# A bank per feature tile for the small products, their sums formed in attention, and the ends of both layers woven

## The chip, the cores and the metric

One core of a Trainium2 chip runs the whole kernel. The metric is the device time of one execution in microseconds, the median of the runs shown. Names of engines are those of the profile: PE is TensorE's matmul, PEld its weight load, DVE VectorE, ACT ScalarE, POOL GpSimd, SP the engine that issues the DMAs.

## The reference, cut to what matters

Two batches of 768 tokens with 8 heads of 64 go through retention (a linear attention with a decaying state), then through two feed-forward layers without residuals:

```python
state = gamma * state + einsum('bhd,bhe->bhde', k[:, :, t], v[:, :, t])
y[:, :, t] = scale * einsum('bhd,bhde->bhe', q[:, :, t], state)
# x = y as 1536 tokens x 512 features
h = x @ w_in                          # 512 x 2048
x = (h * tanh(softplus(h))) @ w_out   # 2048 x 512
gate = 1 / (1 + exp(-(x @ w_gate)))   # 512 x 1536
out = (gate * (x @ w_val)) @ w_out2   # 1536 x 512
```

Everything is float32.

## The kernel before, in words

**Precision.** A float32 operand is split into two parts of PE's reduced type, a high copy (ACT, line 93) and the low rest (a subtraction on POOL or DVE, line 94; lines 195 and 196 for weights). A product of two operands is three matmuls (`mm3`: high x high, high x low, low x high). So a product over 256 input features is six matmuls of 128x128 weights.

**Tiling.** The 1536 tokens are three chunks of N = 512. The 16 blocks of 128 features of layer 1 and the 12 of layer 2 (gate and value) are taken in pairs of output rows. Chunks 1 and 2 are taken together with a seven-product scheme in place of eight (`pair_steps`): steps p1 to p7, each six matmuls, on sums of the inputs (tiles T1, T2, T3, T4 and the plain blocks B11, B21, B22) and sums of the weights (keys "s", made on POOL by lines 205 to 208). DVE forms the results from the products (lines 340, 345, 356, 365, 370). This is the "main" part; its matmuls are 128x512 and its results lie in four PSUM banks named "h". Chunk 0 is treated alike within itself: its two halves of H = 256 tokens form the pair. This is the "side" part; the profile names its products "hx", its matmuls are 128x256, its input sums are the tiles Y, and the profile prints YT for them. The inputs B11, B21, T4 and B22 of the side part are regions of the tile xc. In the old kernel all four side results lie in one PSUM tile "x" of two banks (line 388): bank 0 holds b1 and bA, bank 1 holds bB and b2, and a finished feature is read across both.

**After a product.** In layer 1, ACT applies Mish (line 429); in layer 2, ACT takes the gate's sigmoid (line 434) and DVE multiplies (line 438). The result is split into high and low (tile g). The output sums ("o", `o1` in layer 1, `o2` in layer 2) are six matmuls each over a pair of features in one of two PSUM banks, added to the accumulator of the chunk by DVE (lines 453 and 467), the first of a layer copied by ACT (lines 451 and 465).

**Order.** PE's order is the program's. Until attention's last block, all engines keep the program's order (`InOrder`); behind it the scheduler orders ACT, DVE and POOL from a simulation when it builds the program, and each engine then works through its own list in order. Attention runs in twelve blocks (`blocks`, lines 622 to 639): in block j come the scores of j+1, a decode step of the weights (`pump`), the state and output of j, POOL's preparation of j+2 (vp, og), the loads, and from block 4 on one plain product of layer 1's first four features ("dense"). Behind attention come output sums of chunk 0, plain products of chunk 2, output sums of chunk 1, and then the rounds: `three` issues main step k, side step k-1 and a share of the output sums of the round before (line 524). At k = 6 the last two side steps, p4 and p3, stand right behind each other. `weave` (line 515) spreads a list over another.

**Weights** come as packed words by SP's DMAs (two staging buffers), are decoded by ACT and DVE (lines 104 to 107), and are put into the rings "w" (7 buffers), "o" (4) and "q" (2) as they come free.

**Lines that the steps touch.** Side input sums of layer 1: line 670, once attention's buffers have gone. End of layer 1: lines 685 to 691, round 7's side part alone with four output sums, then its main part with eight, four of which (`out1(L1 - 1, 0, 4)`) join two pairs of features in one group of 12 matmuls; then `put_plain` (splits of chunk 0 for layer 2). Layer 2: lines 692 to 713, with rounds 2 to 10 in `three` and round 11's side and main parts one behind the other.

Of the kernel before, what the change touches and what calls it, by code (L numbers as in the profile page):

```python
# [23 lines left out]
def kernel(ctx, tc, qk, nv, w1i, w1o, w2g, w2v, w2o, ma_in, og_in, sg_in, ck_in, out):  # L24
# [52 lines left out]
    rings = {r: ctx.enter_context(tc.tile_pool(name="ring_" + r, bufs=n)) for r, n in RINGS.items()}  # L77
# [12 lines left out]
    y_t = {"B11": xc_t[:, :2, :, :H], "B21": xc_t[:, 2:, :, :H], "T4": xc_t[:, :2, :, H:], "B22": xc_t[:, 2:, :, H:]}  # L90
# [86 lines left out]
    def room(ring):  # L177
        own = owner[ring]
        n = len(own)
        return n < RINGS[ring] or left[own[n - RINGS[ring]]] == 0  # L180
# [94 lines left out]
    def put_sums(x0, x1, bt, cols, eng):  # L275

        def new(n):
            return up.tile([P, cols], F32, tag="u" if cols == N else "v", name=n)
# [22 lines left out]
    def side_sums():  # L301
        return put_sums(acc_t[0][:, :, :H], acc_t[0][:, :, H:], y_t, H, pool)
# [8 lines left out]
    def pair_steps(key, cols, bt, bank, done, late=False):  # L311
# [16 lines left out]
        def u(n):  # L328
            r[n] = up.tile([P, cols], F32, tag="u" if cols == N else "v", name=n)
            return r[n]  # L330
# [44 lines left out]
    PLACE = {(0, 0): "b1", (0, 1): "bB", (1, 0): "bA", (1, 1): "b2"}  # L375
# [5 lines left out]
    def side_steps(key, done):  # L381

        x = []
# [14 lines left out]
    def plain_steps(key, done, halves=None, own=False):  # L398

        x = []  # L400

        def one(i):
            if not own:
                o = hbank()
            elif "wide" not in hx:
                o = hbank() if i else hx["pool"].tile([P, N], F32, tag="x", name="hx")
            else:
                if not x:
                    x.append(hx["pool"].tile([P, 2, N], F32, tag="x", name="hx"))
                o = x[0][:, i]  # L410
# [113 lines left out]
    def three(main, side, outs, n=7):  # L524

        q = len(outs)
        for k in range(7):
# [5 lines left out]
            run(outs[(q * k + n - 1) // n:(q * k + q + n - 1) // n])  # L533


    with ExitStack() as actx:
# [4 lines left out]
        hx["pool"] = actx.enter_context(tc.tile_pool(name="ps_e", bufs=1, space=PSUM))  # L541
# [79 lines left out]

        def blocks(j0, dense, made):

            for j in range(j0, j0 + SPC):
# [12 lines left out]
                if dense:  # L637
                    dense.pop(0)()
            run(dense)
# [21 lines left out]
    dcs = ctx.enter_context(tc.tile_pool(name="dcs", bufs=1))  # L661
    ps_x = ctx.enter_context(tc.tile_pool(name="ps_x", bufs=1, space=PSUM))
    hx["pool"] = hx["wide"] = ps_x
# [3 lines left out]
    for n in ("T1", "T2", "T3"):  # L667
        y_t[n] = big2.tile([P, 2, 2, H], F32R, tag="y" + n, name="Y" + n)

    put_t4(side_sums(), y_t, pool)  # L670
# [24 lines left out]
    ts = side_sums()  # L695
    run(plain2(1))
    put_t4(ts, y_t, pool)
# [3 lines left out]
    for f in range(2, FF2):  # L701
# [4 lines left out]
        if f < FF2 - 1:  # L706
            three(seq(main_steps((2, f), done)), seq(side_steps((2, f), done)), rest[:n])
        else:
# [60 lines left out]
```

## Time and profile before

| | |
|---|---|
| median of 3 runs | 659.43 us (657.8 to 659.87) |
| profiled execution | 659.44 us, span 657.4 us |
| PE busy | 596.8 us (91%) |
| PEld busy | 495.1 us (75%) |
| DVE busy | 413.0 us (63%) |
| ACT busy | 295.0 us (45%) |
| POOL busy | 350.7 us (53%) |
| mean granted clock of TensorE | 0.966 |

Times of the trace are microseconds from the span's start. A row of the timeline gives start, duration, engine, line, operation, what it writes and reads, the shapes, the count, and in brackets the idle time of the engine just before it with what ended it. Matmuls are pipelined and their ends are modelled, so the spacing of starts is the better measure of a matmul's cost. The granted clock is 1.0 for 2.4 GHz and 0.5 for 1.2 GHz.

### The profile page before, as it was taken

To read this page: it belongs to the slowest core of one execution; us is meant where nothing else is said; L and a number is where in the kernel's file an instruction comes from. 1 tells how busy PE (TensorE), PEld (TensorE's weight loads), DVE (VectorE), ACT (ScalarE), POOL (GpSimd) and SP (SyncE) were. 2 spreads that over 40 slices of the span, in tenths; PEclk is the share of its full clock that TensorE was granted. 3 is DMA by queue.
4 is the path that set the end of the run, shared out by engine and by line. 5 is a ranking of instruction groups with operands and counts; after the bars stand their busy time and mean duration, and the time that the engine had idled before them with its cause. 6 is when DMAs were issued, how large, how long until landed. Compare 5 with 4: busy or idle time off the path is not lost.

```text
span 657.4 us, 8752 instructions
## 1 busy us (share of the span) xinstructions
PE 596.8 (91%) x3342; PEld 495.1 (75%) x3342; DVE 413.0 (63%) x581; ACT 295.0 (45%) x533; POOL 350.7 (53%) x299
## 2 busy tenths in 40 slices
PE   8999676797999999988978988999999999998897
PEld 7888565586878787877856766888888888887786
DVE  4899797127647474647578584457667666555255
ACT  1465736338353535345455473653453353331110
POOL 4375684229474747246793695745665575451000
PEclk9999989797999999999998996999999999999799
DMA  9982212004212020104130041013102221000004
GB/s 351 370 294 71 92 65 90 7 8 150 69 33 97 32 97 32 65 0 129 33 95 1 17 141 68 33 57 103 64 33 97 64 66 65 0 1 1 0 33 160
DMA packets 15593, 52.30 MB, mean 80 GB/s; under 512 B 1984, under 2 KB 2112, under 8 KB 15552
## 3 DMA queue, kind: packets, MB, share of 16 engines
q1 hardware_dynamic: 14976, 51.39, 22.6%
q8 instruction: 26, 0.43, 0.3%
q10 hardware_dynamic: 576, 0.36, 0.2%
q14 instruction: 15, 0.12, 0.1%
HBM read 48.60 MB, written 3.15 MB: 79 GB/s over the span
## 4 chain that ended last, share of the span: by engine, by line
PE 61%; DVE 14%; POOL 11%; DMA 5%; ACT 4%; issue 4%; SPq 0%; DVEq 0%; ACTq 0%; POOLq 0%
PE o L68 27%; PE h L68 22%; PE hx L68 11%; POOL g L94 3%; DMA raw<-w1i 3%; POOL ww L196 2%; POOL wo L196 2%; DVE T L94 1%; DVE a L68 1%; DVE v L68 1%; DVE raw L68 1%; DMA raw<-w2o 1%; DVE h L370 1%; DVE v L107 1%; DMA qk_t<-qk 1%
## 5 line engine op out<-in xcount | busy, mean ns | idle before, releaser
L68 PE MATMUL o<-g,wo 128*128 128x512 f32 x576 | 146.1, 403 | 25.6 <-ACT acc L451 19.2
L94 POOL TENSOR_TENSOR g<-e,g 128x512 fp32r<-128x512 f32 x74 | 104.3, 1414 | 86.9 <-ACT g L93 82.5
L68 PEld LDWEIGHTS o<-g,wo 128*128 128x128 f32 x576 | 109.4, 195 | 50.7 <-ACT acc L451 20.4
L68 PE MATMUL o<-wo,g 128*128 128x512 f32 x432 | 113.1, 399 | 6.0 <-POOL g L94 3.4
L68 PEld LDWEIGHTS o<-wo,g 128*128 128x128 f32 x432 | 79.9, 193 | 22.2 <-POOL g L94 4.6
L68 PE MATMUL h<-B,ww 128*128 128x512 f32 x372 | 95.9, 395 | 0.0
L196 POOL TENSOR_TENSOR ww<-s,ww 128x512 fp32r<-128x512 f32 x32 | 43.2, 1350 | 97.5 <-ACT ww L195 97.5
L68 PE MATMUL h<-T,ww 128*128 128x512 f32 x360 | 92.6, 394 | 0.8 <-DVE u L345 0.8
L68 PEld LDWEIGHTS h<-B,ww 128*128 128x128 f32 x372 | 69.6, 190 | 14.9 <-DVE h L356 0.4
L68 PEld LDWEIGHTS h<-T,ww 128*128 128x128 f32 x360 | 68.2, 190 | 15.6 <-DVE u L345 1.4
L68 PE MATMUL hx<-xc,ww 128*128 128x256 f32 (+1 forms) x336 | 58.4, 313 | 19.3 <-ACT e L429 11.3
L106 DVE SCALAR_TENSOR_TENSOR raw<-raw 128x512 int32<-128x512 int32 x59 | 54.4, 922 | 32.8 <-ACT raw L104 32.7
L107 DVE SCALAR_TENSOR_TENSOR v<-v,raw 128x512 int32<-128x512 int32 x59 | 59.4, 1007 | 23.5 <-ACT v L105 23.1
L68 PEld LDWEIGHTS hx<-xc,ww 128*128 128x128 f32 x336 | 50.4, 197 | 28.8 <-ACT e L429 13.1
L104 ACT ACTIVATE raw<-raw 128x512 int32<-128x512 uint8 x59 | 39.5, 670 | 70.0 <-DMA raw<-w1i 18.9
L453 DVE TENSOR_TENSOR acc<-o,acc 128x512 f32<-128x512 f32 x68 | 46.1, 684 | 28.5 <-PE o L68 28.4
L467 DVE TENSOR_TENSOR acc<-o,acc 128x512 f32<-128x512 f32 x60 | 41.2, 686 | 31.6 <-PE o L68 31.5
L93 ACT ACTIVATE g<-e 128x512 fp32r<-128x512 f32 x77 | 47.9, 625 | 17.3 <-DVE e L438 16.8
L105 ACT ACTIVATE v<-raw 128x512 f32<-128x512 f32 x59 | 39.3, 666 | 34.1 <-POOL s L208 17.7
L68 PEld LDWEIGHTS hx<-YT,ww 128*128 128x128 f32 x288 | 41.5, 196 | 7.7 <-ACT s L335 1.8
L196 POOL TENSOR_TENSOR wo<-v,wo 128x512 fp32r<-128x512 f32 x24 | 35.6, 1486 | 21.7 <-ACT wo L195 21.7
L68 PE MATMUL hx<-YT,ww 128*128 128x256 f32 x288 | 44.0, 290 | 2.6 <-ACT s L335 1.4
(102 smaller groups left out, 790.4 us busy)
## 6 DMA issues: line engine op xcount, KB each, us to landing
raw<-w1i SPq DMA_DIRECT2D x16, 512.0 KB, 3.4
raw<-w1o SPq DMA_DIRECT2D x16, 512.0 KB, 3.3
qk_t<-qk SPq DMA_DIRECT2D x12, 512.0 KB, 5.9
nv_t<-nv SPq DMA_DIRECT2D x12, 512.0 KB, 6.8
raw<-w2g SPq DMA_DIRECT2D x12, 512.0 KB, 3.3
raw<-w2v SPq DMA_DIRECT2D x12, 512.0 KB, 3.3
raw<-w2o SPq DMA_DIRECT2D x12, 512.0 KB, 3.3
out<-acc SPq DMA_DIRECT2D x12, 256.0 KB, 2.0
```

The source lines that it names most:

```text
L68: i = call(**kw)
L93: act.activation(out=hi, in_=raw, func=AF.Copy)
L94: eng.tensor_tensor(out=lo, in0=raw, in1=hi.bitcast(F32), op=ALU.subtract)
L104: act.activation(out=low, in_=rest, func=AF.Copy, scale=1.0 / 32, bias=-15.5 / 32)
L105: act.activation(out=v, in_=high.bitcast(F32), func=AF.Copy, scale=2.0 ** -112)
L106: dve.scalar_tensor_tensor(out=low, in0=high, scalar=SIGN, in1=low, op0=ALU.bitwise_and, op1=ALU.bitwise_or)
L107: dve.scalar_tensor_tensor(out=b, in0=b, scalar=3, in1=low, op0=ALU.logical_shift_left, op1=ALU.bitwise_or)
L196: late_lo.append(lambda: lo_eng["w"].tensor_tensor(out=lo, in0=v, in1=hi.bitcast(F32), op=ALU.subtract))
L370: dve.tensor_tensor(out=r["bB"], in0=r["bB"], in1=r["u2"], op=ALU.add)
L453: dve.tensor_tensor(out=acc, in0=o, in1=acc, op=ALU.add)
L467: dve.tensor_tensor(out=acc, in0=o, in1=acc, op=ALU.add)
```

## The change

There are five edits.

1. The side part's four results get a tile and a bank for each feature of the pair: x0 holds b1 and bB, x1 holds bA and b2. A finished feature is one whole bank. The plain products use the same two tiles.
2. The side input sums of layer 1 are formed in attention. `side_sums` now returns steps that run on POOL (with high copies on ACT); two steps follow each of blocks 5 to 9. Their tiles Y lie in memory that exists from the start, with scratch of their own (`upv`), and the ring "q" is made only after attention.
3. Layer 1's last round runs in `three` with the eight output sums of chunks 1 and 2, followed by `out1(L1 - 1, 0)` and `out1(L1, 0)` as groups of six matmuls.
4. In layer 2's round 2 the four output sums start at step 3.
5. Layer 2's last round runs in `three` with three output sums; what is left follows, then chunks 1, 0 and 2.

```diff
-    y_t = {"B11": xc_t[:, :2, :, :H], ...}
+    y_t = {n: big.tile([P, 2, 2, H], F32R, name="Y" + n) for n in ("T1", "T2", "T3")}
+    y_t |= {"B11": xc_t[:, :2, :, :H], ...}
...
     def side_sums():
-        return put_sums(acc_t[0][:, :, :H], acc_t[0][:, :, H:], y_t, H, pool)
+        x0, x1 = acc_t[0][:, :, :H], acc_t[0][:, :, H:]
+        t = {}
+        def form(n, k, in0, in1, to=None):
+            if to is None:
+                to = upv.tile([P, H], F32, tag="u", name="ty")
+            pool.tensor_tensor(out=to, in0=in0, in1=in1, op=ALU.subtract)
+            t[n, k] = to
+            if n != "T4":
+                low(n, k)
+        def low(n, k):
+            split(t[n, k], y_t[n][:, k, 0], y_t[n][:, k, 1], pool)
+        steps = []
+        for k in range(2):
+            steps += [lambda k=k: form("T1", k, x1[:, k], x0[:, k]),
+                      lambda k=k: form("T2", k, x1[:, 2 + k], t["T1", k]),
+                      lambda k=k: form("T4", k, x0[:, 2 + k], t["T2", k], t["T2", k]),
+                      lambda k=k: form("T3", k, x1[:, 2 + k], x1[:, k], t["T1", k])]
+        return steps + [lambda k=k: low("T4", k) for k in range(2)]
...
         def bank(n):
-            if not x:
-                x.append(hx["pool"].tile([P, 2, 2, H], F32, tag="x", name="hx"))
-            return x[0][:, int(n[1] in "B2"), int(n[1] in "A2")]
+            m, c = SPOT[n]
+            if m not in x:
+                x[m] = hx["pool"].tile([P, N], F32, tag=f"x{m}", name="hx")
+            return x[m][:, c * H:c * H + H]
...
-                done(m, 0, lambda m: x[0][:, :, m])
+                done(m, 0, lambda m: x[m])
...
-    def three(main, side, outs, n=7):
+    def three(main, side, outs, n=7, after=0):
...
-            run(outs[(q * k + n - 1) // n:(q * k + q + n - 1) // n])
+            run(outs[max(q * (k - after) + n - 1, 0) // n:max(q * (k - after + 1) + n - 1, 0) // n])
...
+        ys = side_sums()
...
+                if j >= SPC + 1:
+                    run(ys[:2])
+                    del ys[:2]
...
-    put_t4(side_sums(), y_t, pool)
...
-    for i in range(I0, L1):
-        three(seq(main_steps((1, i), mish_of(i))), seq(side_steps((1, i), mish_of(i))), rest, 3 if i == I0 else 7)
+    for i in range(I0, L1 + 1):
+        n = len(rest) if i < L1 else 8
+        three(seq(main_steps((1, i), mish_of(i))), seq(side_steps((1, i), mish_of(i))), rest[:n], 3 if i == I0 else 7)
+        run(rest[n:])
         rest = out1(i, 1) + out1(i, 2) + out1(i, 0)
-    weave(seq(side_steps((1, L1), mish_of(L1))), rest[:4])
-    weave(seq(main_steps((1, L1), mish_of(L1))), rest[4:8] + out1(L1 - 1, 0, 4))
+    run(out1(L1, 0))
...
-        if f < FF2 - 1:
-            three(seq(main_steps((2, f), done)), seq(side_steps((2, f), done)), rest[:n])
-        else:
+        if f == FF2 - 1:
             lo_eng["g"] = dve
-            weave(seq(side_steps((2, f), done)), rest[:3])
-            weave(seq(main_steps((2, f), done)), rest[3:6] + out2(f // 2, 0))
+            n = 3
+        three(seq(main_steps((2, f), done)), seq(side_steps((2, f), done)), rest[:n], 4 if f == 2 else 7, 3 if f == 2 else 0)
         rest = rest[n:]
-    run(out2(FF2 // 2 - 1, 1), out2(FF2 // 2 - 1, 2))
+    run(rest, out2(FF2 // 2 - 1, 1), out2(FF2 // 2 - 1, 0), out2(FF2 // 2 - 1, 2))
```

## Rows read from the trace of the kernel before

**Rows 1.** Windows: stretch, its length, busy us per engine (instructions), PEclk, DMA share, GB/s.
```profile
28.50:71.00 42.50, 42.50 (x469) 34.44 (x469) 37.39 (x47) 24.68 (x46) 22.78 (x17) 1.00 0.51 179
71.00:127.70 56.70, 37.52 (x146) 29.78 (x145) 40.96 (x44) 30.14 (x59) 34.89 (x31) 0.85 0.20 65
...
288.80:306.00 17.20, 13.73 (x79) 11.44 (x80) 10.45 (x16) 10.45 (x19) 15.79 (x13) 1.00 0.29 93
306.00:350.90 44.90, 38.45 (x163) 30.24 (x162) 31.09 (x42) 23.06 (x43) 33.49 (x30) 0.99 0.19 59
...
605.50:641.10 35.60, 31.48 (x144) 26.27 (x145) 15.15 (x25) 5.46 (x10) 2.53 (x2) 0.90 0.04 15
```

**Rows 2.** Timeline of PE, one step of a woven round in layer 2.
```profile
585.45 1.52 PE L68 MATMUL h<-T,ww 128*128 128x512 f32 x6
586.81 0.88 PE L68 MATMUL hx<-xc,ww 128*128 128x256 f32 x6
587.52 1.55 PE L68 MATMUL o<-wo,g 128*128 128x512 f32 x6
```

**Rows 3.** Timeline of PE, p4, p3 and what follows at a round's end, layer 2.
```profile
580.49 0.87 PE L68 MATMUL hx<-xc,wq 128*128 128x256 f32 x6
...
581.89 0.98 PE L68 MATMUL hx<-xc,ww 128*128 128x256 f32 x6 [0.53 <-DVE hx L365]
...
582.70 0.63 PE L68 MATMUL h<-B,ww 128*128 128x512 f32 x2
```

**Rows 4.** Waits of PE: us in total, times, longest.
```profile
PE o L68 <- ACT acc L451: 19.2, 3, 10.2
PE hx L68 <- ACT e L429: 11.3, 6, 3.5
...
PE hx L68 <- DVE hx L365: 5.3, 10, 0.5
```

**Rows 5.** Timeline, layer 1: the ends of rounds 2 and 6.
```profile
156.20 1.65 PE L68 MATMUL hx<-xc,ww 128*128 128x256 f32 x6 [3.52 <-ACT e L429]
...
157.64 2.76 PE L68 MATMUL h<-B,ww 128*128 128x512 f32 x6
...
286.68 0.87 PE L68 MATMUL hx<-xc,wq 128*128 128x256 f32 x6
...
288.81 0.98 PE L68 MATMUL hx<-xc,ww 128*128 128x256 f32 x6 [1.26 <-ACT e L429]
```

**Rows 6.** Timeline of PE behind attention, the longest idle time.
```profile
119.76 8.11 PE L68 MATMUL o<-g,wo 128*128 128x512 f32 x24 [10.24 <-ACT acc L451]
```

**Rows 7.** Timeline of DVE behind attention, one operation beside POOL's work and without.
```profile
102.71 1.22 DVE L106 SCALAR_TENSOR_TENSOR raw<-raw 128x512 int32<-128x512 int32 x1
...
105.66 0.68 DVE L106 SCALAR_TENSOR_TENSOR raw<-raw 128x512 int32<-128x512 int32 x1
```

**Rows 8.** Groups by shape: busy us, mean ns, idle before; attention's lines read L68.
```profile
L68 POOL TENSOR_TENSOR vp<-nv_t,ck 128x512 f32<-128x512 f32 x12 | 14.7, 1221 | 13.8 <-DMA nv_t<-nv 13.1 <-PE sc L68 0.7
...
L94 POOL TENSOR_TENSOR YT<-t,YT 128x256 fp32r<-128x256 f32 x12 | 13.5, 1134 | 0.0
...
L68 POOL TENSOR_TENSOR g<-e,g 128x512 fp32r<-128x512 f32 x7 | 9.9, 1415 | 16.5 <-ACT g L68 16.5
...
L93 ACT ACTIVATE YT<-t 128x256 fp32r<-128x256 f32 x12 | 4.9, 412 | 5.0 <-POOL t L286 2.3 <-POOL t L284 2.0 <-POOL t L290 0.6
```

**Rows 9.** Timeline of PE, the end of layer 1: two waits.
```profile
303.77 0.97 PE L68 MATMUL hx<-xc,ww 128*128 128x256 f32 x6 [2.09 <-ACT e L429]
...
349.07 2.06 PE L68 MATMUL o<-g,wo 128*128 128x512 f32 x6 [2.99 <-DVE acc L453]
```

**Rows 10.** Timeline of PE and POOL, the output sum open at round 2 of layer 2.
```profile
391.29 0.84 PE L68 MATMUL o<-wo,g 128*128 128x512 f32 x3
...
398.83 0.79 PE L68 MATMUL o<-wo,g 128*128 128x512 f32 x1 [2.86 <-POOL g L94]
...
392.40 3.46 POOL L196 TENSOR_TENSOR ww<-s,ww 128x512 fp32r<-128x512 f32 x2
```

More of the change, by code (lines that the diff above doesn't have):

```diff
@@ L76 @@
     big = ctx.enter_context(tc.tile_pool(name="big", bufs=1))
-    rings = {r: ctx.enter_context(tc.tile_pool(name="ring_" + r, bufs=n)) for r, n in RINGS.items()}
+    rings = {r: ctx.enter_context(tc.tile_pool(name="ring_" + r, bufs=RINGS[r])) for r in "wo"}
+    upv = ctx.enter_context(tc.tile_pool(name="upv", bufs=3))
     stg = ctx.enter_context(tc.tile_pool(name="stg", bufs=STG))
@@ L179, in room @@
         n = len(own)
-        return n < RINGS[ring] or left[own[n - RINGS[ring]]] == 0
+        return ring in rings and (n < RINGS[ring] or left[own[n - RINGS[ring]]] == 0)
     def slot(key):
@@ L277, in new @@
         def new(n):
-            return up.tile([P, cols], F32, tag="u" if cols == N else "v", name=n)
+            return (up if cols == N else upv).tile([P, cols], F32, tag="u", name=n)
         sub = eng.tensor_tensor
@@ L328, in u @@
         def u(n):
-            r[n] = up.tile([P, cols], F32, tag="u" if cols == N else "v", name=n)
+            r[n] = (up if cols == N else upv).tile([P, cols], F32, tag="u", name=n)
             return r[n]
@@ L373, in pair_steps @@
         return [p1, p5, p2, p6, p7, p4, p3] if late else [p1, p6, p7, p5, p2, p4, p3]
-    PLACE = {(0, 0): "b1", (0, 1): "bB", (1, 0): "bA", (1, 1): "b2"}
+    SPOT = {"b1": (0, 0), "bB": (0, 1), "bA": (1, 0), "b2": (1, 1)}
+    PLACE = {v: k for k, v in SPOT.items()}
     def main_steps(key, done, late=False):
@@ L393, in half @@
             if (m, 1 - c) in ready:
-                done(m, 0, lambda m: x[0][:, :, m])
+                done(m, 0, lambda m: x[m])
         return pair_steps(key, H, y_t, bank, half)
     def plain_steps(key, done, halves=None, own=False):
-        x = []
         def one(i):
[L403 to L406, printed above, removed]
-            else:
-                if not x:
-                    x.append(hx["pool"].tile([P, 2, N], F32, tag="x", name="hx"))
-                o = x[0][:, i]
+            o = hx["pool"].tile([P, N], F32, tag=f"x{i}", name="hx") if own and i in hx["own"] else hbank()
             w = weight(("a", *key, i))
@@ L540 @@
         ps_s = actx.enter_context(tc.tile_pool(name="ps_s", bufs=1, space=PSUM))
-        hx["pool"] = actx.enter_context(tc.tile_pool(name="ps_e", bufs=1, space=PSUM))
+        hx["pool"], hx["own"] = actx.enter_context(tc.tile_pool(name="ps_e", bufs=1, space=PSUM)), (0,)
         ma = ac.tile([P, 1, P], F32, name="ma")
@@ L661 @@
     dcs = ctx.enter_context(tc.tile_pool(name="dcs", bufs=1))
+    rings["q"] = ctx.enter_context(tc.tile_pool(name="ring_q", bufs=RINGS["q"]))
     ps_x = ctx.enter_context(tc.tile_pool(name="ps_x", bufs=1, space=PSUM))
-    hx["pool"] = hx["wide"] = ps_x
+    hx["pool"], hx["own"] = ps_x, (0, 1)
     lo_eng["dcs"] = dcs
@@ L666 @@
         b_t[n] = big2.tile([P, 2, 2, N], F32R, tag=n, name=n)
-    for n in ("T1", "T2", "T3"):
-        y_t[n] = big2.tile([P, 2, 2, H], F32R, tag="y" + n, name="Y" + n)
-    put_t4(side_sums(), y_t, pool)
     put_block("T4", 2, 0)
@@ L694 @@
         put_block("B22", 2, 2)
-    ts = side_sums()
-    run(plain2(1))
-    put_t4(ts, y_t, pool)
+    ys = side_sums()
+    run(ys[:8], plain2(1), ys[8:])
     weave(seq(main_steps((2, 0), glu_of(0), True)), out2(0, 0))
```

5 lines of the change are left out of this document (2 added, 3 removed).

## The prediction

> **What bounds the kernel now.** I read the windows by stage first, then the waits of PE, then PE's timeline around each wait. TensorE is the engine that sets the end: it computes or stands still, and hardly anything runs after it. In the steady parts it is nearly gapless. Six matmuls of 128x512 take 1.36 us from start to start, six of 128x256 (a product of the feature tile, "hx") 0.71 us [rows 2]. So 0.227 us is one wide matmul, and what a stage takes beyond its matmuls is loss. Five places of loss are touched by the change. First, 71 to 127.7: 144 wide matmuls are 32.7 us of work in a stage of 56.7, at a mean granted clock of 0.85 [rows 1]. Second, one wait per round at the last feature-tile product, in both layers [rows 3 to 5]. Third, the end of layer 1, 288.8 to 350.9. Fourth, the start of the woven rounds of layer 2, near 395 to 399. Fifth, the end of layer 2, 605.5 to 641.1. Attention itself (28.5 to 71) has PE busy for all of its 42.5 us, DVE for 37.4, POOL for 22.8 [rows 1].
>
> The profiled execution took 659.44 us around a span of 657.4 (2.0 outside it), the median is 659.43. So sums made on the span's rows may be taken from 659.4 directly.
>
> **A. A bank per feature tile, layer 1.** In the old layout one two-bank tile held all four partial products, and step p3 (which writes bB) waited until ACT's Mish (line 429) had read the finished half with bA and b2 in it. PE's waits list six such waits, 11.3 us [rows 4]; five stand at the ends of rounds 2 to 6, the sixth in round 7 (part C). In the last of the five, p4 starts at 286.68 and p3 at 288.81: 2.13 us where 0.71 would do, so 1.42 lost by a wait shown as 1.26 [rows 5]; the six matmuls behind a wait take 0.10 more, as in layer 2 [rows 3]. That is 0.26 over the wait. Three others are alike at 1.48 (what the list leaves for them): 3 x 1.74 + 1.52 = 6.7 us. The first, at 156.20, shows 3.52, and PE is at half clock behind it: six wide matmuls last from 157.64 to 160.20, 2.56 instead of 1.36 [rows 5]. Wait, clock and the slow matmuls behind are some 6.7 us; but the sums that follow want copies that POOL makes about then, so I book 3. In the new layout p4 writes tile x1 and p3 tile x0, nothing of x0 is still being read, and p1 of the next round, which does wait for x0's reader, stands several wide products later. A = 9.7, bounds 6 and 13.
>
> **B. The same in layer 2.** There p3 waits for a DVE addition of 0.43 us (line 365): 5.3 us in 10 waits [rows 4]. From p4 to p3 1.40 instead of 0.71, then 0.81 to the next product instead of 0.71 [rows 3]: 0.79 a round. Rounds 2 to 10 are nine: 7.1 us. PE's timeline shows no other idle time in these rounds, so all of it is PE's. Bounds 6 and 7.5.
>
> **C. The end of layer 1.** Before, the feature tile of round 7 ran alone with four output sums. With the last hx product and sum of round 6 that is eight hx (5.7) and five sums (6.8), 12.5 us of work in the 17.2 from 288.8 to 306 [rows 1]; 4.7 lost, 2.09 of it in one wait [rows 9]. Woven, each step has a wide product beside it and that goes. What follows is dearer: four output sums that were one group of 12 matmuls become two of six, which gives DVE four more additions of about 0.68 (2.7 us), and chunk 0 of the accumulator is complete only just ahead of the sums of chunks 1 and 2, where before a whole woven pass lay behind it. The splits of put_plain and POOL's side sums thus fall into fewer microseconds, in a stage where PE already waits for DVE (2.99 us at 349.07 [rows 9], 8 us in all from 306 to 350.9: 27 groups of 1.36 are 36.7 of 44.9) and where POOL was busy for 15.8 of 17.2 and then 33.5 of 44.9 us [rows 1]. I let the boundary give back 2.5. C = 2, bounds -5 (that loss grows by 9) and +6 (it shrinks a little).
>
> **D. Round 2 of layer 2.** The four output sums of chunk 1 start three steps later. Before, the first of them began at 391.29 and stood open until 398.83, the last wait being 2.86 us for a low copy of POOL [rows 10]; six matmuls that take 1.36 us. Now PE goes on to p6, which wants the weight sum that POOL copies from 392.40 to 395.86, two of them, so the first is there at about 394.1 [rows 10], where PE comes at 391.3. It idles 3 us and starts p6 at 394.2 instead of 399.4, with one output sum (1.36) still to do. That is 3.9; as PE idles less, I count 1 for matmuls that ran at half clock behind the old wait. D = 5, bounds 1 and 9.
>
> **E. The end of layer 2.** From 605.5 to 641.1 PE has eight hx products (one is round 10's p3), seven wide ones and ten output sums: 8 x 0.71 + 17 x 1.36 = 28.8 of 35.6 us [rows 1]. The 6.8 are the lone feature tile's chain, product, DVE or ACT, next product, again with the clock down (0.90). Woven, I book 6.5, bounds 5 and 7. Behind it stand rest, chunk 1, chunk 0, chunk 2: the feature tile's last gate has over 9 us of sums to hide in, chunk 2's last more. The output DMAs on SP are the same twelve in another order, one per 1.36 us; the end behind the last matmul stays.
>
> **F. Side sums in attention.** Eight subtractions and eight low copies of 128x256 on POOL, mean 1.13 us for the copies [rows 8], some 18 us, and eight copies on ACT, move from behind attention into blocks 5 to 9. What they leave: beside POOL a DVE operation takes 1.22 us, without it 0.68 [rows 7], and 16 x 0.54 = 8.6 us of DVE time go from a stage in which PE waited 19.2 us for ACT's copy of an output bank [rows 4], 10.24 of them in one wait with a half-clock stretch behind [rows 6]. ACT stood there in its own order behind decodes and high copies that hung on DVE and POOL. Nothing in the trace shows ACT's new order; the ends are 0 and 24 (all the loss, 56.7 - 32.7). I take 9, near the DVE time freed. What they cost: nothing by the sum, since POOL idles 19.7 us of attention. By the block it doesn't fit: a block is 42.5 / 7 = 6.1 us, POOL holds vp 1.22, an og about like it and a low copy of 1.42 in it [rows 8], and four more of 1.13 with two hand-overs to ACT make 9.3 (about 8 in every second block). Over four blocks that is 10 us of lag, less the block by which vp is made ahead: 5. The new waits: ACT's high copy waits for POOL's subtraction, and behind it stand the decode of the next weight and the copy of the state that PE wants a block later; POOL's low copy waits for ACT, and behind it stand vp and og. Bounds 0 and 12. F = 9 - 5 = +4, from -7 to +17.
>
> The Trainium skill ("SBUF — State Buffer", section "Who interferes with whom") says that a DVE instruction with two SBUF inputs and a POOL instruction that reads SBUF exclude each other, and the second blocks until the first is done. The rows agree that they slow each other, but by 0.54 an operation [rows 7], about half of POOL's span. By the rule, 16 x 1.13 = 18 us would be added to DVE in attention, by the rows 8.6; DVE has 5.1 idle there.
>
> **Without price.** Layer 2's side sums are the same instructions in the same order. The ring "q" opens only after attention, so one decode step is put off by one product; the weights for round 2 are first used some 30 us of matmuls later, which hides it; if not, it costs one piece, about 3 us, in F's bounds. The smaller tiles of put_sums change pools, not number.
>
> **The sum.** 9.7 + 7.1 + 2 + 5 + 6.5 + 4 = 34.3; 659.4 - 34.3 = 625.
>
> **Rivals.** (1) Only the steady waits and the last end are gained: the sums give in attention what they take behind it, and C and D run into POOL, which is nearly full at 288.8 to 306. 659.4 - 9.7 - 7.1 - 6.5 = 636. For it: POOL's window there; against it: the 19.2 us behind attention. (2) The stage after attention closes almost to PE's own time: 19 instead of 9, and C about 4.5: 612. For it: DVE is that stage's busiest helper, 41 of 56.7 us; against it: raw weights come in one by one, and ACT's order is fixed ahead. (3) The banks don't do what they say, because p3 meets the next wait on the spot: without A and B 642. Against it: p3 reads and writes nothing that line 365 or 429 touches. (4) POOL and DVE exclude each other for their full spans in attention: 18 - 5.1 = 13 instead of 5, so 633. The skill's rule would have it so; the 0.54 speaks against it. (5) Slower than before: in attention every one of the 16 POOL operations and 8 ACT copies runs in series with PE, because ACT's state copy and POOL's vp stand behind them: 16 x 1.13 + 8 x 0.41 = 21.4 us [rows 8], decodes come late by as much, and the stage behind keeps its 24 us of loss. With C at its -5 and D at 1, 659.4 - 23.3 + 21.4 + 5 - 1 = 661.5. It decides when attention ends later than about 90 instead of 71. POOL's 19.7 idle us speak against it.
>
> **How the numbers follow.** Forecast 0.50, rival 1 0.22, rival 2 0.12, rival 4 0.06, rival 3 0.05, slower 0.03, no change 0.02. The predicted time is the forecast's, 625. The range runs from 609 (rival 2 with A's upper end) to 642 (rival 3; the forecast with F at its lower end and C below nothing), leaving out about 0.13. A measurement of this kernel can tell about 0.3%, 2 us, from no change: faster 0.95, same 0.02, slower 0.03.
>
> **What would show it.** A and B: no idle time ahead of hx on lines 429 and 365, rounds of about 31 and 22.8 us. C: gapless products in round 7, then PE waiting for line 453's additions. D: no wait of an output sum in round 2, one of about 3 us ahead of p6. E: the last round as dense as the others. F: attention's end at about 76, fewer DVE operations of 1.22 behind it, the first product of round 2 about 4 us earlier. I am wrong if attention ends past 83, or if ACT's copies keep PE waiting 19 us behind it.

## The result, and the profile after

The changed kernel takes 629.98 us (median, 628.73 to 630.53) against 659.52 for the kernel before on the same chip: a ratio of 0.9554, 95% interval [0.9533, 0.9576], a gain of 29.4 us where 34.3 were summed. The profiled execution has a span of 628.2 us at a mean granted clock of 0.978. PE is busy for 591.5 us (94%), ACT for 291.3, DVE for 409.1, POOL for 346.5.

The experiments below ran on several chips, and each ratio is to the kernel before on the same chip, so ratios are compared and not times.

Where the 29.2 us between the two spans come from is read by setting the starts of the same matmuls against each other in PE's two timelines. The third column is the kernel before with the new banks alone, an experiment below.

| stretch of PE's order | before, us | banks alone | after | change − before |
|---|---|---|---|---|
| start to the first output sum (attention) | 71.22 | 71.20 | 82.06 | +10.84 |
| to the first product of round 2 | 56.49 | 55.87 | 46.28 | −10.21 |
| to the output sum behind round 6's p3 | 161.91 | 154.62 | 153.34 | −8.57 |
| to layer 2's first product | 61.31 | 57.31 | 56.82 | −4.49 |
| to round 3 of layer 2 | 69.09 | 66.79 | 60.12 | −8.97 |
| round 3 to the end of round 10 | 186.3 | 180.8 | 186.1 | −0.2 |
| round 11 and what follows | 51.1 | 46.2 | 43.5 | −7.6 |

Windows of the changed kernel by stage; length, busy us of PE, PEld, DVE, ACT, POOL (instructions), PEclk, DMA share, GB/s. They answer [rows 1].

```profile
28.50:82.06 53.56, 47.08 (x470) 37.99 (x469) 36.30 (x46) 25.61 (x51) 34.22 (x32) 0.90 0.40 142
82.06:128.34 46.28, 37.84 (x146) 29.87 (x144) 36.85 (x45) 28.84 (x54) 19.54 (x15) 0.89 0.25 80
281.68:338.50 56.82, 50.92 (x237) 40.53 (x235) 43.46 (x62) 35.37 (x64) 49.06 (x42) 1.00 0.22 75
584.75:612.00 27.25, 27.25 (x141) 23.10 (x140) 16.17 (x27) 6.33 (x12) 2.54 (x2) 1.00 0.03 10
```

Attention, where PE was busy for all of its time at full clock, now has 6.5 us of idle PE at 0.90. The stage behind it is 10.21 us shorter, nearly the 10.84 that attention is longer. The window of the last round and the first output sums behind it has no idle PE at all.

PE's waits, changed kernel: us in total, times, longest. They answer [rows 4].

```profile
PE o L68 <- ACT acc L467: 7.3, 2, 3.8
PE st L68 <- POOL YT L68: 5.6, 2, 3.6
PE o L68 <- POOL g L96: 4.5, 4, 2.4
PE o L68 <- DVE acc L469: 4.5, 5, 1.4
PE hx L68 <- DVE u L363: 3.8, 3, 3.1
```

The 11.3 us for ACT's Mish and the 5.3 for DVE's addition are gone. The 19.2 us for ACT's copy of an output bank are 7.3. New are the state matmul's waits in attention; those for line 363 (line 340 in the kernel before, where one wait of 0.6 us stood) are longer.

PE at a round's end, changed kernel, layer 2, then layer 1; they answer [rows 3] and [rows 5].

```profile
583.32 0.88 PE L68 MATMUL hx<-xc,wq 128*128 128x256 f32 x6
584.03 0.88 PE L68 MATMUL hx<-xc,ww 128*128 128x256 f32 x6
584.75 1.55 PE L68 MATMUL h<-B,ww 128*128 128x512 f32 x6
...
280.25 0.88 PE L68 MATMUL hx<-xc,wq 128*128 128x256 f32 x6
280.96 0.88 PE L68 MATMUL hx<-xc,ww 128*128 128x256 f32 x6
281.68 1.55 PE L68 MATMUL o<-g,wo 128*128 128x512 f32 x6
```

From p4 to p3 0.71, to the next product 0.72: PE's own pace in both layers.

### What attention lost

ACT's timeline in attention, changed kernel (the bracket: idle time ahead and its releaser), and then PE's.

```profile
39.48 0.42 ACT L68 ACTIVATE YT<-ty 128x256 fp32r<-128x256 f32 x1 [2.10 <-POOL ty L68]
41.41 0.42 ACT L68 ACTIVATE YT<-ty 128x256 fp32r<-128x256 f32 x1 [1.51 <-POOL ty L68]
41.73 0.64 ACT L68 ACTIVATE raw<-raw 128x512 int32<-128x512 uint8 x1
42.28 0.65 ACT L68 ACTIVATE v<-raw 128x512 f32<-128x512 f32 x1
42.84 0.36 ACT L68 ACTIVATE s<-st 128x256 f32<-128x256 f32 x1
```
```profile
43.30 0.69 PE L68 MATMUL st<-vp,nv_t 128*64 128x64 f32 x16 [2.02 <-POOL YT L68]
43.79 1.80 PE L68 MATMUL ao<-a,vp 128*64 128x128 f32 x16
45.52 1.97 PE L68 MATMUL ao<-qk_t,s 64*64 64x128 f32 x16
...
62.82 1.12 PE L68 MATMUL st<-vp,nv_t 128*64 128x64 f32 x16 [3.58 <-POOL YT L68]
...
67.48 1.82 PE L68 MATMUL h<-B,ww 128*128 128x512 f32 x6
```

The bracket names POOL, but the operation that ends just before `st` starts is ACT's copy of the state (42.84 + 0.36 = 43.20; at the second wait 62.34 + 0.37 = 62.71). ACT stood 2.10 and 1.51 us for POOL's subtractions. Behind its Y copies came, in its own order, a decode and that state copy, whose bank the next `st` needs. Ahead of the first wait POOL's subtraction (from 38.71) had in turn stood behind the low copy of g in POOL's order (from 37.46), which had waited 0.99 us for ACT. There are two such waits of PE and one of 0.88 for DVE: 6.5 us. Behind each long one the clock is down; windows of the changed kernel, columns as above:

```profile
43.70:47.42 3.72, 3.72 (x42) 3.06 (x37) 3.48 (x5) 1.74 (x3) 2.73 (x3) 0.54 0.37 141
...
62.82:67.50 4.68, 4.68 (x49) 4.02 (x49) 4.58 (x5) 1.74 (x3) 3.28 (x4) 0.50 0.31 112
```

From `st` to the wide product behind it PE takes 4.12 and 4.66 us, where the kernel before had 2.51 in a like block (41.22 to 43.73): 3.8 more. Together that is 10.3 of the 10.84 us.

### What came up in round 3 of layer 2

PE, then DVE and ACT, changed kernel.

```profile
406.87 1.55 PE L68 MATMUL h<-T,ww 128*128 128x512 f32 x6
411.48 0.98 PE L68 MATMUL hx<-YT,ww 128*128 128x256 f32 x6 [3.06 <-DVE u L363]
412.30 2.50 PE L68 MATMUL o<-wo,g 128*128 128x512 f32 x6
```
```profile
410.40 0.69 DVE L108 SCALAR_TENSOR_TENSOR raw<-raw 128x512 int32<-128x512 int32 x1 [1.59 <-ACT raw L106]
411.01 0.41 DVE L363 TENSOR_TENSOR u<-hx,s 128x256 f32<-128x256 f32 x1
```
```profile
409.70 0.67 ACT L106 ACTIVATE raw<-raw 128x512 int32<-128x512 uint8 x1 [1.74 <-DMA raw<-w2v]
```

p7 needs DVE's 0.41 us sum of p6's result. DVE stands at a decode ahead of it, which waits for ACT's half, which waits for a weight's DMA. A wait at another product has taken the place of the one that was moved.

### The profile page after: what moved, and what is told of

The parts are those of the page before. It is cut to its first block, busy times and chain, and to the rows that moved or that the text cites. A ratio compares the mean times of both kernels' runs of the same rounds, so it can differ in the third digit from the quotient of the medians.

```text
span 628.2 us, 8737 instructions
## 1 busy us (share of the span) xinstructions
PE 591.5 (94%) x3342; PEld 492.6 (78%) x3342; DVE 409.1 (65%) x585; ACT 291.3 (46%) x533; POOL 346.5 (55%) x299
## 3 DMA queue, kind: packets, MB, share of 16 engines
q1 hardware_dynamic: 14976, 51.39, 23.4%
## 4 chain that ended last, share of the span: by engine, by line
PE 60%; DVE 14%; POOL 10%; ACT 7%; DMA 6%; issue 3%; SPq 0%; DVEq 0%; ACTq 0%; POOLq 0%
PE o L68 28%; PE h L68 20%; PE hx L68 11%; DVE v L109 3%; DMA raw<-w1i 2%; POOL ww L198 2%; DVE T L96 2%; POOL g L96 2%; DVE v L68 1%; DMA raw<-w2v 1%; DVE raw L108 1%; DVE raw L68 1%; DMA qk_t<-qk 1%; POOL ty L311 1%; POOL g L68 1%
## 5 line engine op out<-in xcount | busy, mean ns | idle before, releaser
L68 PE MATMUL o<-g,wo 128*128 128x512 f32 x576 | 147.3, 405 | 17.3 <-ACT acc L467 7.3
L68 PEld LDWEIGHTS o<-g,wo 128*128 128x128 f32 x576 | 109.0, 195 | 44.1 <-ACT acc L467 8.2
L68 PE MATMUL o<-wo,g 128*128 128x512 f32 x432 | 110.0, 395 | 0.3 <-POOL g L96 0.3
L68 PE MATMUL h<-B,ww 128*128 128x512 f32 x372 | 95.6, 394 | 0.0
L68 PE MATMUL h<-T,ww 128*128 128x512 f32 x360 | 91.9, 392 | 2.7 <-DVE e L454 1.0
L68 PEld LDWEIGHTS o<-wo,g 128*128 128x128 f32 x432 | 78.7, 190 | 15.3 <-POOL g L96 0.7
L68 PEld LDWEIGHTS h<-T,ww 128*128 128x128 f32 x360 | 67.4, 189 | 17.9 <-DVE e L454 1.5
L68 PEld LDWEIGHTS h<-B,ww 128*128 128x128 f32 x372 | 69.6, 190 | 15.0 <-issue 0.5
L108 DVE SCALAR_TENSOR_TENSOR raw<-raw 128x512 int32<-128x512 int32 x59 | 56.0, 948 | 34.3 <-ACT raw L106 33.8
L469 DVE TENSOR_TENSOR acc<-o,acc 128x512 f32<-128x512 f32 x72 | 48.8, 686 | 32.3 <-PE o L68 32.3
L109 DVE SCALAR_TENSOR_TENSOR v<-v,raw 128x512 int32<-128x512 int32 x59 | 60.9, 1032 | 13.9 <-ACT v L107 12.8
L483 DVE TENSOR_TENSOR acc<-o,acc 128x512 f32<-128x512 f32 x60 | 41.3, 688 | 31.0 <-PE o L68 30.9
L68 PE MATMUL hx<-xc,ww 128*128 128x256 f32 (+1 forms) x336 | 54.1, 299 | 0.3 <-DVE xc L68 0.3
L68 PEld LDWEIGHTS hx<-xc,ww 128*128 128x128 f32 x336 | 48.8, 190 | 5.2 <-DVE xc L68 0.7
L68 PEld LDWEIGHTS hx<-YT,ww 128*128 128x128 f32 x288 | 40.7, 190 | 8.6 <-DVE u L363 5.0
L68 PE MATMUL hx<-YT,ww 128*128 128x256 f32 x288 | 42.4, 283 | 3.8 <-DVE u L363 3.8
L198 POOL TENSOR_TENSOR wo<-v,wo 128x512 fp32r<-128x512 f32 x24 | 33.4, 1395 | 22.5 <-ACT wo L197 22.5
L107 ACT ACTIVATE v<-raw 128x512 f32<-128x512 f32 x59 | 39.4, 668 | 12.6 <-POOL s L210 5.7
```

What stands on the lines that cost most here:

```text
L68: i = call(**kw)
L107: act.activation(out=v, in_=high.bitcast(F32), func=AF.Copy, scale=2.0 ** -112)
L108: dve.scalar_tensor_tensor(out=low, in0=high, scalar=SIGN, in1=low, op0=ALU.bitwise_and, op1=ALU.bitwise_or)
L109: dve.scalar_tensor_tensor(out=b, in0=b, scalar=3, in1=low, op0=ALU.logical_shift_left, op1=ALU.bitwise_or)
L198: late_lo.append(lambda: lo_eng["w"].tensor_tensor(out=lo, in0=v, in1=hi.bitcast(F32), op=ALU.subtract))
L469: dve.tensor_tensor(out=acc, in0=o, in1=acc, op=ALU.add)
```

## The experiments

Where a run undoes one part of the changed kernel, its worth is its ratio to before less 0.9554, times 659.5. A ratio's interval is ±1.3 to ±3 us, and a difference of two ratios is uncertain by about 2 to 3.5 us.

### The old two-bank tile in the changed kernel

```diff
-                x[m] = hx["pool"].tile([P, N], F32, tag=f"x{m}", name="hx")
-            return x[m][:, c * H:c * H + H]
+                x.append(hx["pool"].tile([P, 2, 2, H], F32, tag="x", name="hx"))
+            return x[0][:, int(n[1] in "B2"), int(n[1] in "A2")]
```

> The changed kernel with the old two-bank tile for the four side results, all else as changed. Theory: p3 waits at every round's end as before: 8.6 us in layer 1's rounds 2 to 6 (of them 1.8 in round 2), one more wait of about 1.5 in round 7, 0.79 in each of some ten rounds of layer 2; 630 + 8.6 + 1.5 + 7.9 = 647 to 649. Rival: part of it only moves to the next wait, because weights and low copies come no sooner; 637 to 641.

646.04 us, ratio 0.9788 [0.9752, 0.9824]: 15.4 us dearer. PE's waits in this kernel:

```profile
PE hx L68 <- ACT e L453: 10.5, 6, 3.5
...
PE hx L68 <- DVE hx L388: 5.8, 10, 1.0
```

Both waits of [rows 4] are back, 10.5 us for 11.3 and 5.8 for 5.3. So they come from the shared tile. In layer 2 what p3 waits for is an addition to bA, which lay in bank 0, while p3 writes bB in bank 1: there the two share the tile and no bank. The edit gives each feature a tile and a bank at once, so no run here shows what a bank of its own is worth beside a tile of its own.

### The kernel before with the new banks alone

> The kernel before with a bank per feature tile of the side part and nothing else. The prediction's A and B are 9.7 and 7.1 us; undoing the banks alone in the changed kernel cost 16 us. Theory: the banks' worth doesn't depend on the other edits, so about 643 us (640 to 646), no wait of a side product on ACT's Mish or on DVE's addition at the rounds' ends, rounds of 22.8 us in layer 2. Rival: the banks need the woven ends and the new order behind attention to pay; alone they give only layer 2's 7 us and part of layer 1's, 649 to 653.

635.23 us, ratio 0.9663 [0.9616, 0.9709]: a gain of 22 us, more than either theory. The table above says where: 7.3 us in layer 1's rounds and 5.5 in layer 2's rounds 3 to 10, somewhat less than A and B booked, but also 2.3 ahead of round 3 of layer 2, 4.0 at the end of layer 1 and 4.9 at the end of layer 2, which the prediction had given to the weaving. PE in this kernel, the lone side part of round 11:

```profile
585.84 0.88 PE L68 MATMUL hx<-xc,ww 128*128 128x256 f32 x6
587.93 0.98 PE L68 MATMUL hx<-xc,ww 128*128 128x256 f32 x6 [1.21 <-ACT e L427]
588.75 0.88 PE L68 MATMUL hx<-YT,ww 128*128 128x256 f32 x6
590.22 0.97 PE L68 MATMUL hx<-YT,ww 128*128 128x256 f32 x6 [0.59 <-DVE u L340]
```

Before, the same lone part waited 1.94, 0.53, 0.59, 0.53 and 0.53 us, with two side products and the output sum behind them at half clock. With the banks there are three waits, 1.21, 0.59 and 0.53. Two rows of the kernel before:

```profile
608.42 0.98 PE L68 MATMUL hx<-xc,ww 128*128 128x256 f32 x6 [1.94 <-DVE e L438]
609.93 1.65 PE L68 MATMUL hx<-YT,ww 128*128 128x256 f32 x6 [0.53 <-ACT s L335]
```

Part of what looked like a chain of dependent products was the shared tile. The other four edits together are worth the remaining 7 us, give or take 3.

### The old ends of the two layers

Layer 1's last side and main part behind each other again:

```diff
-    for i in range(I0, L1 + 1):
-        ...
-    run(out1(L1, 0))
+    for i in range(I0, L1):
+        ...
+    weave(seq(side_steps((1, L1), mish_of(L1))), rest[:4])
+    weave(seq(main_steps((1, L1), mish_of(L1))), rest[4:8] + out1(L1 - 1, 0, 4))
```

> The changed kernel with the old end of layer 1: round 7's side part alone with four output sums, then its main part with eight. Theory: weaving gave what the two traces differ by from round 6's end to the first plain product of layer 2, 4.5 us, so 634 to 635. Rival 1: with a bank per feature tile the lone side part waits less (2.09 and 1.26 of its waits were ACT's Mish), so most of the 4.5 us is the banks': 631 to 632. Rival 2: the old end was better for the stage behind (chunk 0 complete earlier, DVE and POOL with more time for the sums): 627 to 629.

633.4 us, ratio 0.9594 [0.9573, 0.9615]: 2.6 dearer. The waits for line 469's additions are 6.6 us instead of 4.5, the longest 2.97 instead of 1.36: giving chunk 0 its sums as groups of six did not make the boundary worse.

Layer 2's:

```diff
-        if f == FF2 - 1:
+        if f < FF2 - 1:
+            three(...)
+        else:
             lo_eng["g"] = dve
-            n = 3
-        three(...)
+            weave(seq(side_steps((2, f), done)), rest[:3])
+            weave(seq(main_steps((2, f), done)), rest[3:6] + out2(f // 2, 0))
```

> The changed kernel with the old end of layer 2: round 11's side part alone with three output sums, then its main part with seven. Theory: the lone chain (product, DVE or ACT, next product) costs PE what the two traces differ by from round 11 on, 7.6 us less what the banks alone save in it, about 1: 636 to 638. Rival: with the banks the lone part loses little, 631 to 633.

632.89 us, ratio 0.9605 [0.9584, 0.9626]: 3.4 dearer, with lone waits of 1.21, 0.59 and 0.53 us and the matmuls behind them.

### Round 2 of layer 2 with its output sums from step 0

```diff
-        three(..., rest[:n], 4 if f == 2 else 7, 3 if f == 2 else 0)
+        three(..., rest[:n], 7, 0)
```

> The changed kernel with the four output sums of layer 2's round 2 from step 0 on, as before. Theory: the first of them waits for POOL's low copy at the head of the round, with half clock behind; of the 9.0 us by which the changed kernel's round 3 starts sooner after layer 2's first product, 5 to 8 go; the 3.1 us for which round 3 then waits for u2 (DVE behind a decode that waits for its weights' DMA) go too, because PE comes later: 633 to 635. Rival: the wait of round 3 stays, then 636 to 639.

630.58 us, ratio 0.957 [0.9546, 0.9593]: 1.1 dearer, which these runs can't tell from nothing. The time is under both the theory's and the rival's. The wait of 2.86 us of [rows 10] is back, with the one of 2.65 ahead of it, and the wait of 3.06 us in round 3 is gone. The late start is worth what it saves less the wait that it brings up one round later.

### The side sums behind attention

First only the two lines in the blocks were taken out; then also the Y tiles and their scratch were made after attention, since the scheduler had drawn the sums into attention all the same (POOL's first subtraction at 24.69 us).

```diff
-                if j >= SPC + 1:
-                    run(ys[:2])
-                    del ys[:2]
...
+    run(ys)
     put_block("T4", 2, 0)
```

> The changed kernel with the side sums of layer 1 formed behind attention again (their tiles and the later ring q stay). Theory: the sums alone cost attention its 10.8 us and alone gave the 10.2 us behind it, so attention's last product ends near 71 again (first output sum at 71.2), the first product of round 2 starts near 127.7, and the time is 629 to 630, about the changed kernel's. Rival 1: the 10.2 us behind attention come from another order of ACT (Y tiles elsewhere, ring q later) and not from the sums; then attention is short and the stage behind stays short, 619 to 621. Rival 2: the sums' move is a gain on the whole, then over 632.

624.63 us, ratio 0.9469 [0.9443, 0.9494]; the first output sum starts at 77.19. No case foretold this: the sums still stand in attention, in an order of the scheduler's making, and the kernel is 5.6 us faster than the change.

> The changed kernel with the side sums of layer 1 behind attention as in the kernel before: their Y tiles and their scratch come out of memory that attention has held, so nothing of them can start sooner (in the earlier run of this kind the scheduler had put them into attention by itself, from 24.7 us on, as nothing forbade it). Theory: attention ends near 71 to 72, POOL's 16 operations stand again beside DVE's main sums, and the stage from the first output sum to round 2 takes about 57 us instead of 46; the time is 629 to 631, the changed kernel's. Rival: the shorter stage behind attention has nothing to do with the sums (the ring q made later, another order on ACT); then the stage takes 46 to 48 and the time is 618 to 621.

625.24 us, ratio 0.9482 [0.9452, 0.9512]: 4.7 us faster than the change as it stands, between the theory and its rival. Three of the eight subtractions still start at 24.96 to 27.25 us, ahead of the stretch of attention looked at here; the rest, and all splits, stand behind it. Window of this kernel from the first output sum to round 2, and PE's waits:

```profile
72.39:122.59 50.20, 37.23 (x146) 29.79 (x144) 39.90 (x44) 29.62 (x59) 31.29 (x27) 0.86 0.22 74
```
```profile
PE o L68 <- ACT acc L465: 13.0, 2, 8.3
```

With the splits of the sums behind attention the stage takes 50.20 us, so only 3.9 us of its shortening to 46.28 belong to moving them; 6.3 of the way from 56.49 came without. What gave these 6.3 (the ring q made later, another order of ACT) no run shows; the banks alone leave this stage at 55.87. PE still waits 13.0 us for ACT's copies there. Attention ends at 72.39 instead of 82.06. The move costs 9.7 and brings 3.9. Stage ends shift from profile to profile: in the four kernels that keep the changed kernel's sums in attention and undo an edit elsewhere, attention ends between 81.7 and 84.7, and the first product of round 2 starts at 128.4 to 129.1. That product starts at 128.34 in the changed kernel and at 122.59 here, 5.8 us earlier.

### The sums in attention, in another order

The subtractions go ahead of POOL's vp, the high and low copies to the end of a block, so that ACT finds the sums made. Layer 2's side sums are regrouped in the same way.

```diff
+                if j >= SPC + 1:
+                    run(ys[:2])
+                    del ys[:2]
                 at_prep(j + 2)
...
-                if j >= SPC + 1:
-                    run(ys[:2])
-                    del ys[:2]
+                if j >= SPC + 1 and yl:
+                    run(yl.pop(0))
```

> The changed kernel with the same side sums in attention, in another order: POOL's two subtractions of a block stand ahead of vp, the high copies (ACT) and low copies (POOL) at the block's end, so that no high copy on ACT waits for a subtraction that waits for the gate's low copy. Theory: attention's 10.8 us are ACT's queue (the state copy and the decode stand behind a Y copy that waits for POOL) and the half clock that follows the idle time; then PE hardly waits in attention, the first output sum starts at 72 to 75 instead of 82.1, and the time is 621 to 624. Rival 1: POOL has too much to do in a block whatever the order, vp comes late; the first output sum at 79 to 82, time 628 to 630. Rival 2: attention is short, but the stage behind takes it back, because DVE's decodes and main sums end no earlier; first output sum at 72 to 75, round 2 at 127 to 129, time 629 to 631.

623.96 us, ratio 0.9447 [0.9419, 0.9476]: 7.1 faster than the change. Attention ends at 74.56 at full clock; no state matmul waits. The window of attention, and PE in one of its blocks:

```profile
28.50:74.56 46.06, 44.07 (x471) 34.39 (x469) 41.22 (x47) 25.06 (x50) 37.86 (x32) 1.00 0.50 173
```

```profile
46.92 1.16 PE L68 MATMUL sc<-qk_t 64*128 64x128 f32 x16
48.01 0.69 PE L68 MATMUL st<-vp,nv_t 128*64 128x64 f32 x16
48.53 1.04 PE L68 MATMUL ao<-a,vp 128*64 128x128 f32 x16
49.50 1.09 PE L68 MATMUL ao<-qk_t,s 64*64 64x128 f32 x16
```

The work is the same and on the same engines, and the stage behind attention is as short as before (46.34 us). POOL's 16 operations even take longer, 17.0 us in place of 12.6. So most of attention's loss, 7.5 of 10.84 us, was the order, not POOL's load. The run moves steps of ACT and of POOL at once and doesn't tell their orders apart; 3.3 us stay, 2.0 of them in four waits for DVE's copies into B. Against the kernel with the sums behind attention (0.9482) the well-ordered move gains 2.3 us, which these runs can't tell from nothing.

### The waits that are left

All four start from the reordered kernel. First, a priority for ACT's first copies of output sums in layer 1; then these copies, of both layers, on DVE.

```diff
+            with tc.high_priority():
-            act.activation(out=acc, in_=o, func=AF.Copy)
+                act.activation(out=acc, in_=o, func=AF.Copy)
```

> The reordered kernel (high copies at the block's end) with ACT's copies of the first output sums (the accumulator's start, layer 1) at high priority in the scheduler's order. Theory: the two waits behind attention (3.9 and 4.5 us there, with half clock behind) are ACT's order alone, since the bank is full and nothing else is missing; both go and the time is 613 to 617. Rival 1: ACT's order hides a lack of weights; the waits come back at the first products of round 2 (its sums of weights), 621 to 624. Rival 2: the priority moves other work and costs as much, 622 to 626.

621.62 us, ratio 0.9438 [0.9415, 0.9462]. The waits behind attention stand at 3.85 and 4.46 us: the priority did not shorten them, and the ratio is that of the reordered kernel within the noise.

```diff
-            act.activation(out=acc, in_=o, func=AF.Copy)
+            dve.tensor_copy(out=acc, in_=o)
```

> The reordered side sums with the first output sums' copies into the accumulators (layers 1 and 2, 12 of each layer) made by DVE in place of ACT, nothing else. Theory: PE waits behind attention because this copy stands in ACT's order behind decodes that wait for weights; on DVE it stands elsewhere, the waits of 3.85 and 4.53 us go or fall under 1.5, total near 617 to 620. Rival: DVE is the busier engine there and waits for ACT's halves of the same decodes, so the copy is as late on DVE: waits of 3 to 6 us, total 624 to 628. Round 3's wait of 3.21 us should stay in both.

620.87 us, ratio 0.9432 [0.9413, 0.9451]. A wait of 6.57 us at 87.98 for DVE's copy takes the place of the first, the second goes, and a later wait for a low copy grows from 2.41 to 4.32: what was 10.8 us in three waits is 10.9 in two. In the waits the rival is nearer: on DVE the copy is as late. In the time the theory is, but the 1.0 us against the reordered kernel can't be told from nothing. Round 3's wait, which was to stay, is 2.26 instead of 3.21 us.

Then a third staging buffer, with one g buffer less to make room, and its control.

```diff
+    turn = [stg] * STG
...
-        t = stg.tile([P, DM], I64, tag="raw", name="raw")
+        t = turn[0].tile([P, DM], I64, tag="raw", name="raw")
+        turn.append(turn.pop(0))
...
+    turn.append(ctx.enter_context(tc.tile_pool(name="stg2", bufs=1)))
...
-    gp = ctx.enter_context(tc.tile_pool(name="gp", bufs=8))
+    gp = ctx.enter_context(tc.tile_pool(name="gp", bufs=7))
```

> The reordered side sums as before (subtractions ahead of vp, splits at the end of the block, 624.0 us) with a third staging buffer for packed weights, made after attention; to make room for it the g tiles go from 8 buffers to 7. Theory: the two waits behind attention (3.85 and 4.53 us for ACT's copy of an output bank) and the one of round 3 (3.21 us for a DVE addition) are of one kind: ACT or DVE stands in its own order at a decode whose packed weight has not landed (ACT idle 2.79, 2.71 and 1.43 us for such a DMA just ahead of the late copies, 2.15 and 2.02 ahead of round 3's). A weight requested one piece earlier takes most of that away: the waits fall to 1 to 2 us each, total near 617. Rival: the lists of ACT and DVE decide, whatever the weights do (the copies stand behind splits of the input sums): waits within 0.5 us of what they were, total 623 to 625. Second rival: the seventh g buffer is missed and a new wait of high copies comes in every round: over 630.

624.94 us, ratio 0.9495 [0.9467, 0.9523].

> The control of the run with a third staging buffer: only the g tiles go from 8 to 7 buffers. If 7 suffice, 623 to 625 us and the waits of the reordered kernel (3.85, 4.53, 3.21) as they were; if not, a wait per round for g, over 630.

619.81 us, ratio 0.9417 [0.9397, 0.9436], the lowest of this study. Against this control the kernel with the third staging buffer has a second wait behind attention of 1.54 us instead of 3.91, and layer 2 begins 2.2 us earlier. That doesn't show that the wait was due to a late weight: ACT's copy starts at 111.84 us against 111.41, and behind a weight's DMA as before; PE's output sums that fill the two banks start at 105.33 against 102.53, so PE came to the wait later. The first wait stays at 3.31, round 3's goes from 2.31 to 2.81, and two waits of 1.68 and 2.09 us for side additions come up in later rounds. In all it is 5 us slower. Seven g buffers are enough; that they are 2.0 us better than eight (0.9417 against 0.9447) can't be told from nothing. The two traces differ in layer 2: rounds 4 to 10 are all 22.84 us with seven (two are 23.4 with eight), and round 3's wait is shorter, with a second effect. PE in the kernel with eight buffers, then with seven:

```profile
405.35 1.65 PE L68 MATMUL hx<-YT,ww 128*128 128x256 f32 x6 [3.21 <-DVE u L362]
406.79 2.76 PE L68 MATMUL o<-wo,g 128*128 128x512 f32 x6
409.35 2.29 PE L68 MATMUL h<-B,ww 128*128 128x512 f32 x6
```
```profile
402.73 0.98 PE L68 MATMUL hx<-YT,ww 128*128 128x256 f32 x6 [2.31 <-DVE u L362]
403.55 1.55 PE L68 MATMUL o<-wo,g 128*128 128x512 f32 x6
404.94 1.52 PE L68 MATMUL h<-B,ww 128*128 128x512 f32 x6
```

The three groups behind the wait take 6.13 us (granted clock 0.54) or 3.57 (1.00).

## Why the prediction came out as it did

The total fell inside the range, 5 us above the forecast. The terms did not all hold. By the stages of the table, A fell short by 1.1, B and D together by 2.9 and F by 4.6, while C and E came out 3.6 above what was booked: that part of the closeness is luck.

**A and B** (9.7 and 7.1). Undoing the banks costs 15.4 where 16.8 were summed. The mechanism held: p3 no longer waits. Rounds 3 to 6 gained 6.8 us (predicted 6.7). Round 2, up to the second main product behind it, gave 1.8, not the 3 booked: the low copies that the prediction named as next in line do stop PE, where [rows 5] had one wait of 3.52:

```profile
156.25 0.97 PE L68 MATMUL o<-g,wo 128*128 128x512 f32 x3 [0.61 <-POOL g L96]
159.61 3.45 PE L68 MATMUL o<-g,wo 128*128 128x512 f32 x8 [2.39 <-POOL g L96]
```

In layer 2, seven of the eight rounds 3 to 10 run at 22.84 or 23.4 us instead of 23.6; round 3 doesn't.

**C** (2). The stage gave 4.5. PE does wait for chunk additions as forecast (1.10, 0.82, 0.53, 0.70, 1.36 us), but their sum fell; the price of the extra additions was booked too high.

**C and E were put down to the wrong edit.** Both read the lone side part as a chain that only weaving can fill. The banks alone gave back 4.0 of the 4.5 and 4.9 of the 7.6 us. The sum came out because the losses were counted once; what each edit is worth by itself was wrong: the banks are worth 22 us where they come first and 15.4 where they come last.

**D** (5, from 1 to 9). The forecast was an idle time of 3 us ahead of round 2's p6. The wait for the weight sum did not come. PE does stop ahead of p6, but for 1.05 us and for DVE's multiplication (line 454), and 0.86 ahead of p7:

```profile
378.54 1.66 PE L68 MATMUL h<-T,ww 128*128 128x512 f32 x6 [1.05 <-DVE e L454]
```

From layer 2's first product to round 3 PE gained 9.0 us, of which 2.3 come with the banks alone. But the banks-alone kernel does rounds 3 to 10 in 180.8 us and the changed one in 186.1: round 3's wait and its half clock, and two of 0.33 and 0.38 us. By the run that undoes it the net is 1.1, not clear of nothing. The step that failed is "where a stall goes": p6 was looked at, and not which decodes DVE holds one round later.

**F** (+4, from −7). This is the term with the wrong sign. The stage behind attention shortened by 10.2, near the 9 booked, but 6.3 of it come without the sums. Attention lost 10.84, so by stages the term is −0.6, and by the run with the sums behind attention the move costs 4.7. The bounds given, −7 to +17, don't follow from the ends of its parts (0 to 24 less 0 to 12). Behind attention DVE's time fell from 41.0 [rows 1] to 36.9 us, half of the 8.6 assumed; the decode of [rows 7], now line 108, still takes 1.02 us there on average. In attention the loss was 10.8, not 5. The mechanism had been named (ACT's copy waits for POOL's subtraction, with a decode and the state copy behind it), and PE's idle time, 6.5 us, is near the 5 booked; what the sum lacked is the 3.8 us at the lower clock behind the two long stops. Nor did it come as a lag that builds up: PE stops at two products, and between them there is a block without a stop (the state matmul at 51.48).

Rival 4, full exclusion of DVE and POOL, came near in size (633) for the wrong reason. The prediction held against it that 0.54 is half of POOL's 1.13. But 1.13 is POOL's time beside DVE; alone the same shape took 0.73 in the changed kernel. Around [rows 7] the operations of the two engines end in turn, POOL's at 102.24 and 103.38, DVE's at 102.78 and 103.93: they take turns. So the trace agrees here with the Trainium skill ("SBUF — State Buffer", section "Who interferes with whom"), by which a DVE instruction with two SBUF inputs contends with a POOL instruction that reads SBUF. Yet that is not what most of attention's loss was: the run that reorders the same 16 POOL operations takes its end from 82.06 back to 74.56, with POOL and DVE both busier in attention (37.9 and 41.2 us from 28.50 to 74.56) than in the changed kernel (34.2 and 36.3).

**E** (6.5). 7.6 measured; no wait of PE behind 527.2 us. The stretch from 605.5 to 641.1 held nine output sums and not ten (the 144 matmuls of [rows 1] are 24 groups of six, 8 + 7 + 9), so 8.2 us could be won there and not 6.8.

**The rivals.** Slower (5) asked for attention past 90; it ended at 82. Of rival 1 one half is true, that the sums give in attention what they take behind it; its other half, that C and D run into POOL, is not. Of the marks set out beforehand some were met at the edge: attention ends under 83 but past 76, and ACT's copies keep PE 7.3 us, not 19. One was missed: the first product of round 2 was to come about 4 us earlier and came 0.6 later (128.34 for 127.71).

## What to carry to other kernels

A PSUM tile that two results share made waits here where either was read or written, also where the profile showed what looked like a chain of dependent products. Give every result that is finished at its own time its own tile (here a bank each) before reordering anything, and measure that alone. When work is moved into a stage where an engine has idle time, look at the hand-over and not at the idle time: put the producer's step well ahead of the consumer's (here to the head of a block, and the consumer's to its end), since an engine that stands at a copy holds up all that is behind it in its order. A wait removed by a new order is gone only when the round after it has been looked at too.

## What the runs showed of the hardware that was not expected

The same wait had different prices: behind 2.31 us of idle PE the granted clock was 1.00, behind 3.06 and 3.21 us in the same place it was 0.67 and 0.54 over the next three groups, which then cost 1.6 and 2.6 us more. It is not the wait's length alone: in the same place a wait of 2.91 us (layer 2's old end) was followed by 1.00, and one of 2.46 us (the old tile) by 0.67. Nor is it the wait alone elsewhere: in the kernel with the banks alone, waits of 0.60 and 2.40 us (to 158.34) left the six wide matmuls from 161.92 at half clock, 2.56 us instead of 1.36; in the changed kernel, behind waits of 0.61 and 2.39 us, the same six took 1.65. What decides it is open.

A POOL subtraction of 128x256 in attention took 0.73 us in the changed kernel (8 of them, mean 729 to 733 ns), and so did six of the eight low copies (the other two 1.22), against the 1.13 of [rows 8], by which the prediction had costed the move: POOL's own time was 12.6 us and not 18, and still attention lost twice what was booked.
